# Four vector passes instead of five for the softmax exponentials that VectorE computes, 277 such score blocks instead of 228, and new pacing constants

## The chip, the cores and the metric

The kernel runs on one core of a Trainium2 chip. The core's engines are called as in its profile: PE (TensorE, matrix products; its weight loads are listed apart as PEld), ACT (ScalarE), DVE (VectorE), POOL (GpSimd) and SP (SyncE, which here only issues DMAs and waits). Each engine works through its own instructions in order and waits on semaphores for the others. The metric is the device time of one execution in microseconds (us); lower is better.

## The reference, cut to what matters

Two independent parts share one launch, and their outputs stand side by side.

```
# part A: attention, S = 2048, D = 512, 32 heads of 16
qkv = x @ wqkv                      # split in q, k, v per head
p = softmax(q @ k^T * 16 ** -0.5)   # 32 heads x 2048 x 2048
a = concat_heads(p @ v) @ wo

# part B: H3 block, D = 512 channels
kv = (4-tap causal shift of k with shift_k) * v
y  = causal convolution of kv with ssm_k, length 2048 per channel, + kv * ssm_D
b  = q * y
out = concat([a, b], axis=-1)
```

Part A needs 32 x 2048 x 2048 exponentials, 134 million. Part B is a long convolution for each of 512 channels.

## The kernel before, in words

**Score blocks.** A block is 128 keys x 512 queries of one head, so there are 2048 blocks. They are ordered in 32 groups of 64 (16 key tiles times four heads that sit in four 32-row strips of PE). Scores are written to PSUM by `qk_mm` (L675), one matmul per block; the queries are scaled beforehand so that a score x in PSUM means an exponential of 2 to the power x / 128. PSUM has eight banks of 512 fp32 columns: banks 0 to 5 hold scores, one block each, bank 6 (`PVB`) collects the product of the exponentials with V for the running group, bank 7 (`BGB`) serves everything else.

**Steps.** The main loop counts steps T. In even steps the score blocks go to the lower banks and in odd steps to the upper ones, mostly three banks each. `emit_qk` writes the scores of a step; `emit_exp` makes one ACT instruction of all its blocks (L708), which reads two or three neighbouring banks and writes bf16 exponentials to `PT`, a ring of 18 blocks. `pv_step` multiplies the blocks of step T-2 with V (L791), four at a time in the four strips of PE. A bank is free again once ACT has read it.

**Blocks on DVE.** `dve_block` (L719) decides in each step with at least three banks whether one of its blocks goes to DVE instead of ACT. It refuses while the work that waits on DVE is above `BACKLOG` us (5.8), while the fixed-point buffer of four blocks ago is in use, or near the end of a group, where 2.6 x `GAP` is the limit in blocks; there it may take a block of the next group. Such a step's ACT instruction has two banks and not three. `exp_on_dve` (L744) writes the passes, each one instruction on 128 x 512:

- L750: `fx = min(x + FIX_ADD, FIX_HI)`, fp32, PSUM to SBUF. The sum is placed so that its low 16 bits are the fraction f of the exponent, scaled by 2^16, and its value is, to first order, the bit pattern of the bf16 exponential. After it the PSUM bank is free.
- L757, three times: `eh = (eh + A) * f`, the steps of Horner's rule for a quartic in f that corrects the first order; in the first of them `eh` is f itself, read as uint16.
- L762: `PTD = eh * A4 + fx`, written as uint16, which is the bf16 exponential's bits. `PTD` is a ring of five blocks.

The passes after L750 wait in a list, `flow`. `advance` takes from it, in DVE's order, whatever the plan holds to be ready, and at most two blocks' passes are interleaved, so that a pass need not follow directly on the one whose result it reads. Other DVE work is `urgent`: it is put in when its input is due, and `slack` (`S_FX` for L750, 0.45) says how far listed passes may still go ahead of it.

**The convolution.** For each channel PE multiplies shifted windows of the kernel's taps (`WR`) with the values `KV`. Four channels (a quad) take 16 lags of four small matmuls each (`conv_lags`, L961); there are 128 quads, 2048 lags and 8192 matmuls. The windows of a quad are 2 MB, read from a scratch array in HBM by four DMAs on SP's queue, into a ring of four quads: 268 MB in all. The load into a ring place is issued when PE is done with the quad before. `emit_bg` puts lags between the steps' other work: each step adds to an allowance `PACE` x (lags left) / (time left by the plan), held below `RATE` per us and in sum below `CAP`; no more than `LAGS` = 6 are issued in one step, none past the room that PE has before the next scores are due, and a quad is begun only when the plan has its windows landed 1.5 us before (`WAIT`). In the rest of PE's room `warm_up` issues matmuls on zeros (L1166), which keep PE busy and compute nothing.

**The plan.** The whole order of work is fixed when the program is written: each `Eng` keeps a model of its time, `PLAN` (710) is the number of steps that due times are reckoned by, and the other projections (queries, keys, values, the output product) are `jobs` with due steps. On the chip only semaphores hold.

## Time and profile before

Three runs took 840.17, 843.98 and 844.13 us, median 843.98. The profiled execution has a span of 840.8 us from its first to its last instruction; no time of its own beyond the span is listed for it, and the span lies 0.6 us above the fastest run and 3.2 below the median.

| Engine | busy us | share of the span | instructions |
|---|---|---|---|
| ACT | 825.8 | 98% | 726 |
| DVE | 814.7 | 97% | 1392 |
| PE | 792.8 | 94% | 13774 |
| PEld | 333.3 | 40% | 13774 |
| POOL | 77.6 | 9% | 155 |

Busy time counts every moment in which an instruction is under way. Two neighbouring instructions overlap a little, so the duration of one is longer than the distance from its start to the next one's. PE's 792.8 us contain 162.4 us of the matmuls on zeros. The DMA engines moved 291.42 MB, 347 GB/s over the span.

### The profile page before, as it was taken

Reading aid. Unit: us, or ns where it says so; the run is one execution under the profiler, and the core shown is the slowest. Engines: PE = TensorE matmul, PEld = TensorE weight load, DVE = VectorE, ACT = ScalarE, POOL = GpSimd, SP = SyncE. Lnnn points to the kernel's source line nnn. Section 1 sums busy time; section 2 is a strip of 40 time slices with the busy share of each in tenths; the row PEclk is TensorE's granted clock in tenths of the full one; section 3 lists DMA queues with packets and bytes.
Section 4 is the critical chain, followed back from the end, with each engine's and each line's share of the span. In section 5 each row is a group of like instructions: output and inputs, shape, how many; then the busy total and the mean of one; then the engine's idle time right before and its main releaser. Section 6 shows DMA issues by size and latency. Waiting matters only on the chain.

```text
span 840.8 us, 30758 instructions
## 1 busy us (share of the span) xinstructions
PE 792.8 (94%) x13774; PEld 333.3 (40%) x13774; DVE 814.7 (97%) x1392; ACT 825.8 (98%) x726; POOL 77.6 (9%) x155
## 2 busy tenths in 40 slices
PE   8999999999999999999999999999999999999997
PEld 3343334444343434344434334443433333333442
DVE  3999999999999999999999999999999999999996
ACT  6999999999999999999999999999999999999997
POOL 3200220010100101000110010101002020000000
PEclk9999999999999999999999999999999999999999
DMA  9997199999999999999999999999999999999952
GB/s 230 216 310 285 50 371 370 354 347 408 392 408 394 393 402 338 371 326 378 330 379 408 384 340 359 377 405 398 406 408 379 351 394 409 409 316 391 405 200 76
DMA packets 109235, 291.42 MB, mean 347 GB/s; under 512 B 37680, under 2 KB 41648, under 8 KB 108720
## 3 DMA queue, kind: packets, MB, share of 16 engines
q1 hardware_dynamic: 102256, 280.80, 90.6%
q0 software_dynamic: 5648, 8.27, 3.2%
q8 instruction: 109, 1.79, 0.9%
q10 hardware_dynamic: 1200, 0.39, 0.2%
q14 instruction: 22, 0.18, 0.1%
HBM read 276.83 MB, written 6.42 MB: 337 GB/s over the span
## 4 chain that ended last, share of the span: by engine, by line
ACT 92%; PE 3%; DVE 3%; DMA 1%; issue 0%
ACT PT L708 92%; DVE EH L757 2%; PE PS L675 1%; PE PS L791 1%; DMA xT<-in_A_x_dram 1%; PE PS L961 1%; DVE PTD L762 1%; DVE FX L750 1%; PE PS L536 0%; PE PS L415 0%; PE PS L1166 0%; DVE DT L852 0%; ACT QT L920 0%; DVE DTN L863 0%; PE PS L902 0%
## 5 line engine op out<-in xcount | busy, mean ns | idle before, releaser
L708 ACT ACTIVATE PT<-PS 128x1536 bf16<-128x1536 f32 (+2 forms) x721 | 822.9, 1455 | 2.6 <-PE PS L675 2.6
L675 PE MATMUL PS<-QT,KTo 32*128 32x512 bf16 x2048 | 286.6, 384 | 34.6 <-ACT PT L708 6.6
L757 DVE SCALAR_TENSOR_TENSOR EH<-EH,FX 128x512 f32<-128x512 f32 x456 | 305.1, 687 | 0.0
L961 PE MATMUL PS<-WR,KV 128*15 128x128 bf16 (+15 forms) x8192 | 213.4, 219 | 1.1 <-issue 1.1
L791 PE MATMUL PS<-PT,VA 128*32 128x512 bf16 x1820 | 196.8, 389 | 2.0 <-DVE DT L852 0.6
L961 PEld LDWEIGHTS PS<-WR,KV 128*1 128x1 bf16 (+15 forms) x8192 | 144.7, 87 | 82.3 <-issue 47.1
L675 PEld LDWEIGHTS PS<-QT,KTo 32*128 32x128 bf16 x2048 | 72.7, 91 | 234.4 <-ACT PT L708 185.3
L1166 PE MATMUL PS<-IDN,ZW 128*32 128x512 bf16 (+4 forms) x632 | 162.4, 335 | 0.2
L750 DVE TENSOR_SCALAR FX<-PS 128x512 f32<-128x512 f32 x228 | 156.9, 690 | 2.4 <-PE PS L675 1.3
L762 DVE SCALAR_TENSOR_TENSOR PTD<-EH,FX 128x512 uint16<-128x512 f32 x228 | 155.7, 685 | 0.0
L757 DVE SCALAR_TENSOR_TENSOR EH<-FX 128x512 f32<-128x512 uint16 x228 | 155.7, 689 | 0.0
L259 POOL DMA_DIRECT2D QT<-QS x120 | 58.7, 497 | 481.5 <-DVE QS L442 165.7
L791 PEld LDWEIGHTS PS<-PT,VA 128*32 128x32 bf16 x1820 | 47.5, 93 | 108.6 <-issue 97.7
L791 PE MATMUL PS<-PTD,VA 128*32 128x512 bf16 x228 | 68.3, 383 | 0.3 <-DVE PTD L762 0.3
L1166 PEld LDWEIGHTS PS<-IDN,ZW 128*32 128x32 bf16 (+1 forms) x632 | 52.6, 96 | 23.8 <-issue 6.7
L852 DVE STREAM_TRANSPOSE DT<-PS 128x512 f32<-128x512 f32 x32 | 22.9, 716 | 6.2 <-PE PS L791 5.9
L975 DVE CAST YB<-PS 128x512 bf16<-128x512 f32 x32 | 22.0, 688 | 0.8 <-PE PS L961 0.8
L426 PE MATMUL PS<-WKV,xT 128*128 128x128 bf16 x256 | 18.8, 220 | 1.0 <-DVE KTo L451 0.7
L902 PE MATMUL PS<-WKV,OTN 128*128 128x512 bf16 x64 | 19.2, 384 | 0.3 <-DVE OTN L872 0.3
L403 PE MATMUL PS<-xT,WKV 128*128 128x512 bf16 (+1 forms) x64 | 18.1, 377 | 0.6 <-DVE KTo L451 0.5
L791 PEld LDWEIGHTS PS<-PTD,VA 128*32 128x32 bf16 x228 | 17.0, 95 | 2.0 <-DVE PTD L762 0.6
L394 PE MATMUL PS<-xT,WQ 128*128 128x512 bf16 x60 | 17.6, 384 | 0.2 <-DVE VA L473 0.2
(63 smaller groups left out, 211.8 us busy)
## 6 DMA issues: line engine op xcount, KB each, us to landing
WR<-kz_scratch SPq DMA_DIRECT2D x512, 512.0 KB, 8.0
kz_scratch<-WR SPq DMA_DIRECT2D x1, 2176.0 KB, 8.3
QN<-in_B_q_dram POOLq DMA_DIRECT2D x2, 1024.0 KB, 12.6
out_dram<-QN POOLq DMA_DIRECT2D x2, 1024.0 KB, 8.5
QT<-QS POOLq DMA_DIRECT2D x120, 16.0 KB, 5.2
out_dram<-OUTA POOLq DMA_DIRECT2D x12, 128.0 KB, 5.8
QN<-in_B_ssm_k_dram SPq DMA_DIRECT2D x1, 1024.0 KB, 8.5
OTN<-in_B_ssm_k_dram SPq DMA_DIRECT2D x1, 1024.0 KB, 9.1
```

The costliest lines, as they stand in the source:

```text
L259: f(outp, inp).then_inc(dsem.sem, 16)
L675: ins = e.matmul(PS[:, bank, :], lhsT=KTo[32 * s:32 * s + 32, OF[n_] % 2, kt * 128:(kt + 1) * 128], rhs=QT[32 * s:32 * s + 32, n_ // 2 % R ...
L708: h_exp[T] = act.op(lambda e: e.activation(PT[:, p0:p0 + n, :].rearrange("p b f -> p (b f)"), PS[:, banks[0]:banks[0] + n, :].rearrange("p ...
L750: h_f = urgent(lambda e: e.tensor_scalar(fx, PS[:, bank, :], FIX_ADD, FIX_HI, ALU.add, ALU.min), [h, h_last.get(i - R_FX)], slack=S_FX)
L757: st["h"] = dve.op(lambda e: e.scalar_tensor_tensor(eh, src, (A3, A2, A1)[j], frac, ALU.add, ALU.mult), [st["h"], h_last.get(i - R_EH)], u ...
L762: lambda e: e.scalar_tensor_tensor(out16, eh, A4, fx, ALU.mult, ALU.add),
L791: ins = e.matmul(dst, lhsT=w, rhs=rhs, start=(k == 0), stop=(k == KT - 1), tile_position=(0, 32 * s))
L852: h_t = urgent(lambda e: e.transpose(out=dt, in_=PS[:, PVB, :]), [h, h_mul.get(n - 1)], slack=S_T, us=(0.63, 0.751))
L902: ins = e.matmul(PS[:, bank, :], lhsT=OTN[:, PAIRS.index((o, qb)), t * 128:(t + 1) * 128], rhs=WO[:, o, :], start=(o == 0), stop=(o == 3))
L961: ins = e.matmul(PS[32 * c:32 * c + NB - n, BGB, 128 * (kk % 4):128 * (kk % 4) + 128], lhsT=KV[:, qd, n:NB, c], rhs=WR[:, r + c, 128 * (NB ...
L975: hh = urgent(lambda e: e.tensor_copy(YB[:, half, :].rearrange("p (k i) -> p k i", k=4), src), [h, h_yb[0]], slack=S_C, us=V512)
L1166: pe.op(lambda e, s=s, k=k, rhs=rhs, bank=bank, rows=rows, c0=c0, first=first: e.matmul(PS[32 * s:32 * s + rows, bank, c0:c0 + 128 * k], l ...
```

## The change

Horner's quartic becomes two nested quadratics: `y = (f + P1) * f`, `z = (y + P2) * y`, `PTD = z * P3 + fx`. So L757 is issued twice per block and not three times, and a block has four DVE passes and not five. In the second of them both operands and the result are `eh`. ACT's bias moves by 5.016e-5. With the shorter chain and the new constants of the plan, the program gives DVE 277 blocks instead of 228 and ACT the other 1771 instead of 1820. The convolution's allowance grows faster (`PACE`, `RATE`) and may be saved up further (`CAP`); `LAGS`, the most in one step, stays at 6. The other constants touched belong to the plan: how late L750 may come (`S_FX`), the reckoned number of steps (`PLAN`), the limit near a group's end (`GAP`), and the work that may wait on DVE (`BACKLOG`).

```diff
-PACE = 1.05
+PACE = 1.2
...
-EXP_BIAS = (LIFT + 1) * math.log(2.0)
...
-A3, A2, A1 = 255023.64843928182, 77186915383.44943, -6435437372016724.0
-A4 = 9.315941845433171e-20
+P1 = 7.78027265 * 2.0 ** 16
+P2 = -8.78027265 * 2.0 ** 32
+P3 = 4.46542389e-3 * UNIT / 2.0 ** 64
+EXP_BIAS = (LIFT + 1) * math.log(2.0) + 5.016e-5
...
-S_FX = 0.45
+S_FX = 0.55
...
-PLAN = 710
+PLAN = 705
...
-GAP = 8
+GAP = 7
...
-BACKLOG = 5.8
+BACKLOG = 6.0
...
-RATE = 3.4
-CAP = 10.0
+RATE = 3.7
+CAP = 14.0
...
-        def horner(j, us):
+        def square(j, us):
             src = frac if j == 0 else eh
-            st["h"] = dve.op(lambda e: e.scalar_tensor_tensor(eh, src, (A3, A2, A1)[j], frac, ALU.add, ALU.mult),
+            st["h"] = dve.op(lambda e: e.scalar_tensor_tensor(eh, src, (P1, P2)[j], src, ALU.add, ALU.mult),
                              [st["h"], h_last.get(i - R_EH)], us=us)
...
-                lambda e: e.scalar_tensor_tensor(out16, eh, A4, fx, ALU.mult, ALU.add),
+                lambda e: e.scalar_tensor_tensor(out16, eh, P3, fx, ALU.mult, ALU.add),
...
-        flow.append([("p", dep, lambda us: horner(0, us), V512,
-                      lambda: i < R_EH or i - R_EH in h_last)]
-                    + [("p", dep, lambda us, j=j: horner(j, us), V512, lambda: True) for j in (1, 2)]
-                    + [("p", dep, last, V512, lambda: i < R_PTD or i - R_PTD in h_ptd)])
+        flow.append([("p", dep, lambda us: square(0, us), V512,
+                      lambda: i < R_EH or i - R_EH in h_last),
+                     ("p", dep, lambda us: square(1, us), V512, lambda: True),
+                     ("p", dep, last, V512, lambda: i < R_PTD or i - R_PTD in h_ptd)])
```

## The prediction, made before the result was known

> **What bounds the kernel now.** I read the busy shares first, then the chain that ended last, then the groups of instructions by shape, then who waited for whom, and last the stretches of 20 us.

> The page's busy shares and its chain:

> ```profile
> span 840.8 us, 30758 instructions
> PE 792.8 (94%) x13774; PEld 333.3 (40%) x13774; DVE 814.7 (97%) x1392; ACT 825.8 (98%) x726; POOL 77.6 (9%) x155
> ...
> ACT 92%; PE 3%; DVE 3%; DMA 1%; issue 0%
> ```

> ACT carries 92% of the chain. DVE, at 97%, is nearly as full, so both must be counted.

> The groups, shapes kept apart (count, busy us, mean ns, idle before and its releaser):

> ```profile
> L708 ACT ACTIVATE PT<-PS 128x1536 bf16<-128x1536 f32 x372 | 575.2, 1663 | 0.7 <-PE PS L675 0.7
> L708 ACT ACTIVATE PT<-PS 128x1024 bf16<-128x1024 f32 x346 | 395.4, 1229 | 0.4 <-PE PS L675 0.4
> L757 DVE SCALAR_TENSOR_TENSOR EH<-EH,FX 128x512 f32<-128x512 f32 x456 | 305.1, 687 | 0.0
> ...
> L750 DVE TENSOR_SCALAR FX<-PS 128x512 f32<-128x512 f32 x228 | 156.9, 690 | 2.4 <-PE PS L675 1.3
> L762 DVE SCALAR_TENSOR_TENSOR PTD<-EH,FX 128x512 uint16<-128x512 f32 x228 | 155.7, 685 | 0.0
> L757 DVE SCALAR_TENSOR_TENSOR EH<-FX 128x512 f32<-128x512 uint16 x228 | 155.7, 689 | 0.0
> L1166 PE MATMUL PS<-IDN,ZW 128*32 128x512 bf16 x360 | 115.8, 380 | 0.0
> ```

> The reader sees 372 activations of three blocks, 346 of two (three more have four), and five DVE passes per block that all last about the same, whatever they read.

> DVE's order of time, 662 us into the run (start, duration):

> ```profile
> 661.62 0.68 DVE L762 SCALAR_TENSOR_TENSOR PTD<-EH,FX 128x512 uint16<-128x512 f32 x1
> 662.21 0.69 DVE L757 SCALAR_TENSOR_TENSOR EH<-EH,FX 128x512 f32<-128x512 f32 x1
> 662.82 0.69 DVE L757 SCALAR_TENSOR_TENSOR EH<-FX 128x512 f32<-128x512 uint16 x1
> ```

> A pass lasts 0.69 us but the next starts 0.60 us after it: 0.60 is the price of a pass.

> The waits of PE and ACT (us in total, times, longest):

> ```profile
> PEld PS L675 <- ACT PT L708: 185.3, 483, 0.9
> ...
> ACT PT L708 <- PE PS L675: 2.6, 5, 1.5
> ```

> PE waits for ACT 185.3 us, to get a score bank back; ACT waits for PE 2.6. Together with 162.4 us of matmuls on zeros, PE has some 350 us that the plan can give away.

> Stretches of 20 us (PE, PEld, DVE, ACT, POOL busy, granted clock, DMA share, GB/s):

> ```profile
> 480.00:500.00 20.00, 19.42 (x294) 7.17 (x286) 19.95 (x34) 20.00 (x20) 3.88 (x8) 1.00 0.99 353
> ...
> 700.00:720.00 20.00, 19.29 (x359) 7.87 (x356) 19.85 (x36) 20.00 (x19) 1.08 (x2) 1.00 1.03 409
> ...
> 800.00:820.00 20.00, 18.91 (x366) 8.11 (x360) 19.85 (x35) 20.00 (x18) 0.00 (x0) 1.00 0.47 184
> ```

> ACT is solid in all of them; the DMA engines are busy throughout too, with 353 to 409 GB/s, and the convolution's loads end only after 800 us.

> **The change, part by part.** The sum is made against the profiled execution: span 840.8 us, with 9.7 us ahead of the first L708 and 7.1 after the last (it ends at 833.7). Neither end is touched.

> *ACT loses 49 blocks.* From the start times of L708 in the trace, a two-block activation is followed after 904 ns and a three-block one after 1331 (medians), so a block costs 427 ns and an activation 50 ns besides. Before: 1820 x 0.427 + 721 x 0.050 = 777.1 + 36.1 = 813.2 us. The stretch from first to last L708 is 824.0, so 10.7 us are small gaps, in 18 places over 0.15 us and many tiny ones. After: 1771 x 0.427 = 756.2. The number of activations should stay near 721, since a block on DVE takes its bank out of an activation and leaves the step. Bounds: 5 steps fewer, as the reckoned 705 instead of 710 has it, is -0.25 us; 49 steps more, were every further DVE block to keep its bank a step longer, is +2.4. I take 721, nearest to the present mix. ACT: 49 x 0.427 = -20.9 us, all on the path.

> *The gaps.* Two-block activations exceed 904 ns by 23 ns on average, three-block ones 1331 by 7.5. With 49 of the threes turned into twos: 395 x 0.023 + 323 x 0.0075 = 11.5 us, +0.8. Bounds: all gaps gone, -10.7; doubled, since 21 us less of PE's slack remain and the convolution comes in larger portions, +10.7. I take +0.8, because ACT's waits for PE, 2.6 us, are small against 350 us of slack.

> *DVE has 277 x 4 = 1108 passes instead of 228 x 5 = 1140.* 32 fewer at 0.60 us is -19.2. L750, L762 and the first L757 keep their operands; the second L757 reads `eh` on both inputs and writes it, and no row shows one fp32 tensor on both inputs. The nearest rows bound it: L757 with `eh` as input and output, 687 ns, and L757 with f on both inputs, 689. I take 0.60 and bound it by 0.58 and 0.62, the neighbours' spread, 277 x 0.02 = 5.5 us each way. DVE's busy time becomes 795.5. Now it idles 26.1 us: 12.8 in the first 20 us, 7.7 in the last 20.8, 5.6 in between. With the ends kept, DVE alone would need 795.5 + 20.5 = 816.0 us, 4 to 5 less than ACT's path, so it stays second but close. If the pass took 0.62, DVE would need 821.5, about ACT's time.

> *S_FX, GAP, BACKLOG.* L750 may start up to 0.1 us later, so a bank comes back 0.1 us later in at most 277 steps. What hides it: DVE holds its bank while ACT reads two others for 904 ns and then the next step's for at least as long. Without that cover it is 28 us; who waited for L750 in the trace was PE's weight load, 2.7 us in 6 places, so I take 0. GAP lets DVE take blocks 2.6 blocks (about one step) later in a group; a group's closing product then waits for them, behind it the transpose L852, which waited 5.9 us in all. Priced with the gaps above.

> *The convolution.* The lags, their matmuls and the 512 loads stay; only their places move. A quad needed 5.67 us before (first lag 93.6, last 820.3, 128 quads). The span shorter by 20, it must come down to about 5.52. Where loads follow each other closest they land 5.06 to 5.15 us apart per quad, so it fits, by 7%. What the larger allowance takes on PE comes out of L1166 and PE's waits. PE reads no window that has not landed: the smallest distance from landing to first use was 2.8 us, the median 6.6, and no wait of PE names these loads. SP's queue only waits for ring places and issues (0.43 us each), so earlier lags mean earlier issues. POOL's queue, with 120 issues of the queries' copies, gets a busier DMA; these land in 5.2 us (at most 7.9) and are due 24 steps, some 27 us, ahead: nothing.

> [...]

> *Sum.* -20.9 + 0.8 = -20.1 us: 820.7 us against the span. The median lay 3.2 us above the span, so the same difference gives 823.9. I take the middle, 822: two of the three runs were high, the profiled one and the third low. ACT is still first, DVE 4 us behind it.

> **The rivals.**
> 1. *The gaps double.* PE gets shorter steps (904 ns more often) and portions of up to 6 lags more often, and DVE has less than 5 us of idle time inside; each late bank delays ACT. For it: between 194 and 219 us the chain already runs along DVE's passes. Against: the solid ACT rows. 822 + 10.7 = 833.
> 2. *The gaps go.* The new plan might avoid the late places. 822 - 10.7 = 811. Nothing in the profile speaks for it.
> 3. *The windows can't come faster.* From the first issue at 51.4 to the last landing at 810.9 us the loads' mean was 353 GB/s; if troughs such as 480 to 500 us belong to the stream and can't be filled, the last landing stays where it is, and 30 us later the kernel ends: 841 to 844, no change. Against: from 80 to 100 us the DMA engines idle, the ring being full, and 409 GB/s are reached. [...]
> 4. *Slower: PE stalls on windows.* The plan now asks for up to 1.2 x 2048 lags over 708 us, 3.47 per us, more than the 16 per 5.1 us, 3.14, that land at best. So early quads are begun as soon as the plan holds them to be landed. If they land later than planned, PE stops in order, with the next scores behind it, and ACT after about one step. It decides where the stop costs ACT 20.1 / 124 = 0.16 us per quad; at 0.3 us the time is 822 + 37 = 859. Against: the 2.8 us of smallest distance, in stretches where the loads were already back to back.
> 5. *The change does not take hold:* DVE can't carry more than 228 blocks in time, and ACT waits for what it was spared. About 843. Against: 1108 passes are fewer than 1140.

> **How the numbers follow.** The forecast has 0.77; rivals 1 to 5 have 0.11, 0.03, 0.03, 0.04 and 0.02. The forecast's own range is 816 (half of the gaps gone) to 828 (half again as many, on the high kind of run). To leave out no more than 2 in 10 it must reach the doubled gaps: 816 to 833. Half a per cent, 4.2 us, is about what a measurement of this kernel can tell from no change, its runs being 4 us apart. Faster: forecast and rivals 1 and 2, 0.91; within: 3 and 5, 0.05; slower: 4, 0.04.

> **What would show it.** Right: L708 with about 721 instructions, some 395 of them two-block, and some 802 us busy; L757 with 277 + 277 instructions at 0.69 us; ACT still about 92% of the chain; L1166 shrunk by up to 20 us; the last L961 near 800 us or before. Wrong: L961 waiting for `WR` loads, ACT's idle time before L708 above 15 us, L708 counts well above 721, or a second L757 longer than 0.71 us.

## The result and the profile after

The changed kernel takes 833.7 us (median of 4 runs, 827.86 to 834.92), the kernel before 842.96 (4 runs); the ratio is 0.9886, 95% interval 0.985 to 0.9923. So the change makes the kernel faster by 1.1%, 9.3 us, where 822 us and 816 to 833 were forecast. The profiled execution has a span of 832.3 us and took 834.01 in all.

The page of the changed kernel: shares, and the chain that ended last.

```profile
span 832.3 us, 30664 instructions
PE 773.8 (93%) x13668; PEld 327.7 (39%) x13668; DVE 794.8 (95%) x1360; ACT 808.2 (97%) x730; POOL 78.5 (9%) x155
...
ACT 69%; PE 15%; DVE 11%; issue 3%; DMA 2%; POOL 0%; DVEq 0%
```

DVE's 794.8 us were forecast as 795.5. But ACT's part of the chain has fallen from 92% to 69%, and PE, DVE and "issue" stand in its place.

The groups of the changed kernel, shapes kept apart (busy us, mean ns, idle before and releaser):

```profile
L709 ACT ACTIVATE PT<-PS 128x1536 bf16<-128x1536 f32 x316 | 482.0, 1579 | 8.7 <-PE PS L676 8.6
L709 ACT ACTIVATE PT<-PS 128x1024 bf16<-128x1024 f32 x405 | 429.9, 1167 | 3.2 <-PE PS L676 2.7
...
L758 DVE SCALAR_TENSOR_TENSOR EH<-EH 128x512 f32<-128x512 f32 x277 | 186.4, 686 | 0.0
L758 DVE SCALAR_TENSOR_TENSOR EH<-FX 128x512 f32<-128x512 uint16 x277 | 186.3, 689 | 0.0
```

There are 725 activations (three of four blocks and one of a single block besides these). With the same start-to-start times as before (904 and 1331 ns) they need 792.5 us, 20.7 less than before; -20.9 was forecast. The pass that reads `eh` twice lasts 686 ns like every other. The gaps between activations, though, have grown from 10.7 to 24.4 us:

| From 840.8 to 832.3 us of span | us |
|---|---|
| ACT's work, start to start | -20.7 |
| gaps between activations | +13.7 |
| earlier first activation (8.1 instead of 9.7 us) | -1.6 |

The sum, -8.6, is the difference of the spans to 0.1. The first activation came between 8.0 and 10.0 us in the profiles of all kernels here (8.1 in one that differs from the kernel before in its windows alone), so I take the third row for chance. The question is where the 13.7 us come from.

Waits of the changed kernel (us, times, longest):

```profile
ACT PT L709 <- PE PS L676: 12.4, 18, 2.1
...
PE PS L962 <- issue: 10.7, 11, 2.0
```

ACT waits for the scores, and PE, in the midst of its convolution (now L962), for nothing that the profile names. Such a place, in order of time:

```profile
234.80 0.09 PEld L792 LDWEIGHTS PS<-PT,VA 128*32 128x32 bf16 x1 [0.23 <-issue]
...
236.49 0.40 PE L792 MATMUL PS<-PT,VA 128*32 128x512 bf16 x4 [1.62 <-issue]
...
237.43 3.83 ACT L709 ACTIVATE PT<-PS 128x1536 bf16<-128x1536 f32 x3 [0.74 <-PE PS L676]
```

PE loads the first of four weights and then stands still for 1.62 us, inside a group of matmuls of which only the first waits on a semaphore. The next scores come late, ACT idles 0.74 us.

In PE's order of instructions (matmuls, weight loads and its few separate waits, numbered from 0) these places have something in common. The list has every pause over 0.35 us ahead of an instruction that waits on nothing, and the packet of the DMA queue of kind "instruction", 16384 bytes each, that ended before it:

```
pause ends  us    number  mod 256   packet start  end     end to resume
187.85     0.90    5313     193        185.41    186.50      1.35
207.78     0.43    6081     193        205.43    206.54      1.24
236.49     1.60    7105     193        233.93    235.01      1.48
270.97     0.90    8385     193        268.45    269.55      1.43
277.89     1.55    8641     193        275.23    276.31      1.57
406.25     0.85   13505     193        404.03    404.97      1.28
494.57     2.04   16321     193        492.15    493.12      1.45
547.84     0.44   18113     193        545.45    546.59      1.25
554.35     1.72   18369     193        552.05    553.02      1.33
588.02     0.84   19649     193        585.50    586.60      1.43
595.26     0.73   19905     193        592.76    593.84      1.43
```

All eleven (12.0 us) lie at one place of a period of 256 instructions, and each ends 1.2 to 1.6 us after such a packet. A twelfth, 0.84 us at 485 us, lies at the same border ahead of a waiting instruction. The kernel before has three, 1.7 us in all, also at 193 of 256. My reading, which the experiments below test: PE had used up its instructions and waited for the next block of 256, which such a packet brings. The counts in the trace agree: 108 packets of 16384 bytes on that queue, and PE has 27682 instructions, 108 times 256 and 34 more.

By this reading the block that comes is fetched while the running one is used up: a packet starts 3.4 us (median; 95% below 4.9, longest 6.3) after PE enters a block and takes 1.1, and at the pauses above PE goes on 1.4 us later. From the entry that is 5.8 us in the median, while a block lasts 6.95 us (median). Where lags are dense it lasts less: without its pause, under 6 us in 24 cases (with 22.6 lags in the mean, the other blocks with 18.1), before in 8.

After the longest pause PE was also slow, in the stretch behind the pause that ended at 494.57 (PE, PEld, DVE, ACT, POOL, granted clock, DMA share, GB/s):

```profile
496.00:500.00 4.00, 4.00 (x75) 1.79 (x67) 1.79 (x3) 3.02 (x3) 0.00 (x0) 0.61 0.93 266
```

The granted clock was 0.61 in these 4 us, and ACT lost another 1.2 us. From 424 to 428 us it was 0.57, after PE had stood still for 2.4 us for another cause (below, the queries' copies). Behind the other pauses it stayed at 1.00.

With that, ACT's 24.4 us of gaps can be told apart by place. At the twelve border places, each counted from the pause's begin to 2.2 us after its end, they are 10.5 us; between 419 and 430 us 3.1; in the slow stretch behind 496 us 1.2. Outside these places 9.6 us are left. In the kernel before, its three border places have 1.3 us, and 9.4 lie elsewhere.

### The profile page after: what moved, and what is told of

The parts are those of the page before. It is cut to its first block, busy times and chain, and to the rows that moved or that the text cites. A ratio compares the mean times of both kernels' runs of the same rounds, so it can differ in the third digit from the quotient of the medians.

```text
span 832.3 us, 30664 instructions
## 1 busy us (share of the span) xinstructions
PE 773.8 (93%) x13668; PEld 327.7 (39%) x13668; DVE 794.8 (95%) x1360; ACT 808.2 (97%) x730; POOL 78.5 (9%) x155
## 2 busy tenths in 40 slices
DMA packets 109235, 291.41 MB, mean 350 GB/s; under 512 B 37680, under 2 KB 41648, under 8 KB 108720
## 4 chain that ended last, share of the span: by engine, by line
ACT 69%; PE 15%; DVE 11%; issue 3%; DMA 2%; POOL 0%; DVEq 0%
ACT PT L709 69%; PE PS L676 5%; DVE EH L758 4%; PE PS L962 3%; PE PS L792 3%; DVE FX L751 3%; DVE PTD L763 2%; PE PS L1167 1%; DMA QT<-QS 1%; DMA QN<-in_B_k_dram 1%; DMA xT<-in_A_x_dram 1%; PE PS L427 0%; DVE DT L853 0%; POOL QT L260 0%; PE PS L395 0%
## 5 line engine op out<-in xcount | busy, mean ns | idle before, releaser
L709 ACT ACTIVATE PT<-PS 128x1024 bf16<-128x1024 f32 (+2 forms) x725 | 805.2, 1349 | 12.9 <-PE PS L676 12.4
L962 PE MATMUL PS<-WR,KV 128*15 128x128 bf16 (+15 forms) x8192 | 213.0, 220 | 10.8 <-issue 10.7
L751 DVE TENSOR_SCALAR FX<-PS 128x512 f32<-128x512 f32 x277 | 189.1, 689 | 8.6 <-PE PS L676 8.0
L763 DVE SCALAR_TENSOR_TENSOR PTD<-EH,FX 128x512 uint16<-128x512 f32 x277 | 187.5, 685 | 0.1
L758 DVE SCALAR_TENSOR_TENSOR EH<-EH 128x512 f32<-128x512 f32 x277 | 186.4, 686 | 0.0
L758 DVE SCALAR_TENSOR_TENSOR EH<-FX 128x512 f32<-128x512 uint16 x277 | 186.3, 689 | 0.0
L962 PEld LDWEIGHTS PS<-WR,KV 128*15 128x15 bf16 (+15 forms) x8192 | 143.4, 88 | 86.6 <-issue 56.0
L1167 PE MATMUL PS<-IDN,ZW 128*32 128x512 bf16 (+4 forms) x517 | 134.5, 328 | 0.3 <-DVE DT L853 0.2
L792 PE MATMUL PS<-PTD,VA 128*32 128x512 bf16 x277 | 81.3, 383 | 0.3 <-DVE PTD L763 0.3
L1167 PEld LDWEIGHTS PS<-IDN,ZW 128*32 128x32 bf16 (+1 forms) x517 | 43.3, 96 | 26.2 <-issue 11.1
L792 PEld LDWEIGHTS PS<-PTD,VA 128*32 128x32 bf16 x277 | 20.1, 95 | 2.0 <-DVE PTD L763 0.6
L404 PE MATMUL PS<-xT,WKV 128*128 128x512 bf16 (+1 forms) x64 | 18.4, 378 | 1.0 <-DVE KV L462 0.5
```

Of the source, the lines that this page charges most:

```text
L709: h_exp[T] = act.op(lambda e: e.activation(PT[:, p0:p0 + n, :].rearrange("p b f -> p (b f)"), PS[:, banks[0]:banks[0] + n, :].rearrange("p ...
L751: h_f = urgent(lambda e: e.tensor_scalar(fx, PS[:, bank, :], FIX_ADD, FIX_HI, ALU.add, ALU.min), [h, h_last.get(i - R_FX)], slack=S_FX)
L758: st["h"] = dve.op(lambda e: e.scalar_tensor_tensor(eh, src, (P1, P2)[j], src, ALU.add, ALU.mult), [st["h"], h_last.get(i - R_EH)], us=us)
L763: lambda e: e.scalar_tensor_tensor(out16, eh, P3, fx, ALU.mult, ALU.add),
L792: ins = e.matmul(dst, lhsT=w, rhs=rhs, start=(k == 0), stop=(k == KT - 1), tile_position=(0, 32 * s))
L962: ins = e.matmul(PS[32 * c:32 * c + NB - n, BGB, 128 * (kk % 4):128 * (kk % 4) + 128], lhsT=KV[:, qd, n:NB, c], rhs=WR[:, r + c, 128 * (NB ...
```

## The experiments

Three theories were tried. Theory 1: PE's instructions come late, because their fetch queues behind the convolution's windows in the DMA engines and because denser lags use up a block faster. Theory 2: the shorter steps are too tight for PE, DVE and the banks. Theory 3: PE waits for windows that land late. In the figures below, pauses are those of the list above (over 0.35 us, ahead of an instruction without a wait), and gaps are ACT's, over the start-to-start times.

**Half of the windows' traffic, on the changed kernel**

```diff
-            for c in range(4):
+            for c in range(2):
...
-                h_wr[qd] = dma(sp, d_wr[i], WR[:, 4 * i + c, :], src, [h_kzw[0], dep])
+                h_wr[qd] = dma(sp, d_wr[i], WR[:, 4 * i + c, :], src, [h_kzw[0], dep], kb=1024)
...
-                                   rhs=WR[:, r + c, 128 * (NB - 1 - n):128 * (NB - n)],
+                                   rhs=WR[:, r + c % 2, 128 * (NB - 1 - n):128 * (NB - n)],
```

> The changed kernel, but of each quad's four channels only two have their windows loaded (two DMAs of 512 KB instead of four), and the other two channels' matmuls read those same windows; so half of the convolution is not the reference's, while every engine's instructions and their order stay as in the changed kernel. Theory 1 (PE runs out of instructions: the fetch of its next 256 waits in the DMA engines behind the windows): the gaps of PE inside a group of matmuls, 12.8 us in 12 places, fall below 3 us, the fetch's packet starts well under 3 us after PE enters the block before, and the time falls from 833.7 to 820 to 824. Theory 2 (the plan is too tight on PE and DVE, late banks delay ACT): the stream of windows has nothing to do with it, the time stays at 832 to 835. Theory 3 (PE waits for windows that land late): faster as well, 820 to 826; e3 tells it from theory 1.

823.88 us (ratio to the kernel before 0.9761, 0.9722 to 0.98). The DMA traffic of this kernel:

```profile
DMA packets 72369, 157.16 MB, mean 191 GB/s; under 512 B 33584, under 2 KB 37552, under 8 KB 71856
```

and its chain that ended last, by engine:

```profile
ACT 91%; PE 3%; DVE 3%; DMA 1%; issue 1%
```

The fetch's packet starts 1.1 us after PE enters a block (median) instead of 3.4. (43 matmuls are missing in this trace, so PE's instructions were counted by the weight loads, which are complete.) Two pauses are left, 2.1 us, again at 193 of 256, and gaps of 14.0 us. ACT has its 91% of the chain again. That is theory 1's or 3's; theory 2 falls for 10 of the 13.7 us. The gap of 3.1 us at the queries' copies is gone too, so not all of the 10 is the fetch's.

**The same on the kernel before**

The edit is the same.

> The kernel before with the same halving of the windows (two of a quad's four channels loaded, the others read the same). It says what the halving is worth where there is little to cure. Theory 1: PE's gaps inside a group of matmuls were 1.7 us in 3 places and go; the time falls by 1 to 3 us, to 839 to 842. Theory 2: no change, 842 to 844. Theory 3: no change either, since no window landed less than 2.8 us ahead of its use.

840.16 us, ratio 0.9972 (0.9953 to 0.9992): 2.4 us faster by the interval's middle, no pause left, gaps 9.8. Taking the traffic away helps little where blocks were seldom late, so most of the 10 us of the first experiment was the change's own loss.

**Half of the convolution's matmuls, all of the traffic**

```diff
             for n in range(n0, n1):
-                for c in range(4):
+                for c in range(2):
```

> The changed kernel with all windows loaded, but with the convolution's matmuls of two of the four channels left out (8192 to 4096; the four run side by side in PE's strips, so the plan's times stand; half of the convolution's output is missing). PE's instructions fall by some 8192 of 27700. Theory 1: PE needs 256 new instructions less often (mean block time from 7.0 to some 10 us) and the fetch is in time though the DMA engines are as busy as before: gaps inside a group below 2 us, time 820 to 824. Theory 2: what is tight is ACT, DVE and the order of steps, which stay: 830 to 835. Theory 3: the windows land no earlier, so PE waits for them as before: 832 to 835.

822.71 us (ratio 0.975, 0.9709 to 0.9791). This kernel's DMA traffic:

```profile
DMA packets 109203, 290.89 MB, mean 354 GB/s; under 512 B 37680, under 2 KB 41648, under 8 KB 108720
```

and its wait for windows (us, times, longest):

```profile
PEld PS L962 <- DMA WR<-kz_scratch: 8.9, 13, 1.8
```

The DMA engines move as much as in the changed kernel (291.41 MB there) and more per second (350 GB/s there). PE even waits for windows in 13 places, which it did not in the changed kernel. Still there is no pause of the list's kind, 76 packets are fetched instead of 108, a block lasts 10.2 us (median), and the time is 11 us lower. That speaks against theory 3 for the changed kernel and for theory 1: with the same traffic, fewer instructions suffice.

**The new pace alone, on the kernel before**

```diff
-PACE = 1.05
+PACE = 1.2
...
-RATE = 3.4
-CAP = 10.0
+RATE = 3.7
+CAP = 14.0
```

> The kernel before (five passes, 228 blocks) with only the convolution's new pace (PACE 1.2, RATE 3.7, CAP 14). Theory 1: the lags come in denser portions and the DMA engines are full earlier, so PE's blocks of 256 instructions are used up faster and their fetch comes later: gaps inside a group of matmuls rise from 1.7 to 4 to 10 us, and the time from 843 to 846 to 851. Theory 2: the steps stay long and DVE's work the same, so the time stays at 841 to 844. Theory 3: windows are used sooner after landing, 0.5 to 3 us; slower only if PE's waits end with a landing.

849.19 us, ratio 1.0078 (1.0054 to 1.0102): the time that theory 1 expected, but not for its reason. There is one pause, 0.4 us. PE's wait for windows:

```profile
PE PS L961 <- DMA WR<-kz_scratch: 6.9, 6, 3.5
```

Here it is theory 3: the windows are used so soon after landing that PE waits for them, 5.4 of the 6.9 us between 428 and 448 us, where 1 MB of the convolution's output goes out on POOL's queue between its issue at 433.4 and 445.1. ACT's gaps are 17.7 instead of 10.7 us. So the denser pace costs time by itself, through either of two transfers in the same DMA engines (90% busy or more in 34 of the page's 40 slices here, in 35 in the changed kernel); through which, depends on the kernel that it is put in.

**The four passes alone, DVE held to 227 blocks**

All constants as before, and in `dve_block`:

```diff
+        if i >= 228 * T / 715:
+            return None
```

> The four passes alone: the changed kernel's formula with all constants of the plan as before and DVE held to 227 blocks, ACT having 1821. The forecast's first step says that time goes only with ACT's blocks: L708 stays at 813 us of starts plus 10 to 12 of gaps, DVE idles some 130 us more, and the time stays at 840 to 845. Rival: DVE's 97% was itself a bound, late passes caused the gaps, and with 227 passes fewer the gaps shrink: 830 to 836.

845.63 us, ratio 1.0041 (1.0019 to 1.0063), 0.6 us outside what was expected. Shares:

```profile
PE 787.9 (93%) x13786; PEld 330.3 (39%) x13786; DVE 711.3 (84%) x1160; ACT 827.1 (98%) x727; POOL 78.7 (9%) x155
```

DVE has 103 us less to do and nothing is gained: DVE was no bound, and the gain is in ACT's 49 blocks. That it is 3.5 us slower goes with gaps of 14.3 us. The pauses are three, 2.2 us, little more than before. A wait of DVE for the copies of the queries, 6.3 us in 2 places, is among the causes of the gaps; the rest was not followed.

**Two of the three pace constants set back, on the changed kernel**

```diff
-RATE = 3.7
-CAP = 14.0
+RATE = 3.4
+CAP = 10.0
```

> The changed kernel with two of the convolution's three constants set back (RATE 3.4, CAP 10; PACE stays at 1.2, since with 1.05 besides the lags no longer end before the last steps). Theory 1: PE's blocks of 256 instructions are used up a little more slowly, but still often in less than 6 us; gaps at a block's border 5 to 11 us instead of 12, time 827 to 833. Theory 3 (windows): they are used a little later after landing, nothing else: 831 to 835.

831.37 us (0.9865, 0.9836 to 0.9894); seven pauses, 6.5 us, all at the border; gaps 18.4. The time lies in the ranges of theory 1 and theory 3 alike, and its runs (830.28 to 832.09) lie within those of the changed kernel, so only the pauses and gaps speak, and for theory 1: a little less dense, a little less lost.

**A plan that counts PE's instructions**

On top of the last kernel:

```diff
+FETCH = 5.8
+FETCH_AT = 191
+FETCH_REST = 15.0
...
+        if self.ins is not None:
+            c = Count()
+            fn(c)
+            k = (self.ins - FETCH_AT) // 256
+            self.ins += c.n + max(len(waits) - 1, 0)
+            if (self.ins - FETCH_AT) // 256 > k:
+                self.entered = self.t
...
+        soon = pe.entered + FETCH - pe.t
+        if soon > 0:
+            left = min(left, int((256 - (pe.ins - FETCH_AT) % 256 - FETCH_REST * soon) / 8))
```

`Count` calls a group's function with matmuls that only count two instructions each, one for the weights. A lag has eight, and the plan reckons 15 per us for all other work.

> As e6, and the plan counts PE's instructions: for 5.8 us after PE enters a block of 256 it issues no more lags than leave enough of the block for the other work until then. DMA traffic, DVE's and ACT's blocks stay (277 and 1771). Theory 1: the fetch is in time nearly always; gaps at a block's border below 3 us, ACT's gaps 12 to 16 us in all, time 819 to 825, faster than both kernels. Theory 2 (the plan is tight on banks and DVE): as e6, 827 to 835.

824.58 us, ratio 0.9781 (0.9746 to 0.9816), faster than both kernels, and 6.8 us below the kernel without the count, on the same chip (the two profiled executions are 4.5 us apart, 3.7 of it ACT's gaps). DVE has 277 blocks, where the kernel without the count has 276. One block of 256 instructions lasts under 6 us, where the changed kernel had 24, and there is no pause. Its groups of activations (busy us, mean ns, idle before):

```profile
L734 ACT ACTIVATE PT<-PS 128x1536 bf16<-128x1536 f32 x317 | 492.2, 1625 | 1.2 <-PE PS L701 1.1
L734 ACT ACTIVATE PT<-PS 128x1024 bf16<-128x1024 f32 x404 | 439.0, 1201 | 2.7 <-PE PS L701 2.2
```

ACT's wait for the scores (us, times, longest), which was 12.4 us in the changed kernel:

```profile
ACT PT L734 <- PE PS L701: 5.0, 8, 1.7
```

Two of its stretches (PE, PEld, DVE, ACT, POOL, granted clock, DMA share, GB/s):

```profile
260.00:280.00 20.00, 19.23 (x384) 8.16 (x383) 19.94 (x36) 20.00 (x19) 3.81 (x8) 1.00 1.03 399
...
540.00:560.00 20.00, 18.23 (x385) 7.89 (x386) 19.88 (x36) 20.00 (x18) 0.00 (x0) 1.00 1.03 408
```

The same stretches of the changed kernel:

```profile
260.00:280.00 20.00, 16.97 (x354) 7.45 (x345) 17.78 (x32) 18.60 (x18) 3.82 (x8) 1.00 1.03 394
...
540.00:560.00 20.00, 17.33 (x375) 7.91 (x372) 18.66 (x33) 18.40 (x17) 1.90 (x4) 1.00 1.02 375
```

ACT is solid (20.00) where it had lost 1.4 and 1.6 us, with the DMA engines as full. ACT's gaps are 14.7 us.

**PACE alone set back, on the changed kernel**

```diff
-PACE = 1.2
+PACE = 1.05
```

> The changed kernel with PACE alone set back to 1.05 (RATE 3.7, CAP 14 stay). The allowance grows more slowly while many lags are left, but what is saved up can still be spent six at a time. Theory 1: fewer short blocks, gaps at a block's border 4 to 10 us, time 826 to 832. Theory 3: windows are used 1 to 3 us later after landing than in the changed kernel, no wait names them in either, time as the changed kernel's, 831 to 835.

831.28 us (0.9876, 0.9829 to 0.9923), in the ranges of theory 1 and theory 3 alike; the pauses are fewer than theory 1 said, four with 2.5 us, and the gaps are 20.2. Some 4.5 us of them lie between 421 and 428, at one place where the queries' copies come late (below). Its runs (828.93 to 835.28) overlap those of the changed kernel almost wholly, so this run tells little.

Pauses and gaps side by side:

| Kernel | pauses | us | ACT's gaps, us | median us |
|---|---|---|---|---|
| before | 3 | 1.7 | 10.7 | 842.96 |
| changed | 11 | 12.0 | 24.4 | 833.7 |
| before, half the windows | 0 | 0 | 9.8 | 840.16 |
| before, new pace | 1 | 0.4 | 17.7 | 849.19 |
| four passes, 227 blocks | 3 | 2.2 | 14.3 | 845.63 |
| changed, half the windows | 2 | 2.1 | 14.0 | 823.88 |
| changed, half the matmuls | 0 | 0 | 14.7 | 822.71 |
| changed, RATE and CAP as before | 7 | 6.5 | 18.4 | 831.37 |
| the same, instructions counted | 0 | 0 | 14.7 | 824.58 |
| changed, PACE as before | 4 | 2.5 | 20.2 | 831.28 |

Pauses are one cause of gaps among several: the new pace on the kernel before adds its gaps through late windows, and in the last row 4.5 us come from the queries' copies.

## Why the prediction failed, point by point

- *ACT loses 49 blocks, -20.9 us:* right, -20.7. The number of activations, 725 instead of the 721 taken, lies between the bounds, and two-block ones are 405 instead of 395.
- *DVE, second by 4 to 5 us, the new pass at 0.60:* right; 794.8 us busy, the pass 686 ns, and with 227 blocks it idles without any gain.
- *The gaps, +0.8 us:* this step failed. They grew by 13.7, beyond the upper bound of 10.7. The reason given, 350 us of PE's slack against 2.6 us of ACT's waits, counts PE's time, and counts it too high: the 185.3 us are idle time of the weight loads, and in 159 of them PE's matmuls run. PE's own wait for ACT in the kernel before is this:

```profile
PE PS L675 <- ACT PT L708: 6.6, 24, 0.6
```

  PE idled 48.0 us in all, so its slack was nearer to 210 us, still plenty. What ran out was PE's supply of instructions, of which a lag needs eight in 55 ns of the plan's time: 10.5 us of gaps lie at the borders, 1.3 before. Rival 1 had the time, 833, and the wrong mechanism: it put the loss on late banks, short steps and portions of lags. Of these only the portions show a part, through the instructions; outside the places named the gaps are as before, 9.6 and 9.4 us.
- *The convolution, "what the larger allowance takes on PE comes out of L1166 and PE's waits":* true of time (L1167 is down to 134.5 from 162.4 us busy), and the step that should have had a price: packing the same lags more densely cost instruction fetches in time. The profile of before held the sign. In its chain, in order of time, there are three pieces put down to nothing:

```profile
192.05 0.44 issue
...
410.35 0.60 issue
...
617.21 0.64 issue
```

  They belong to the three pauses of before. Pauses that the profile can't name, on the engine whose instructions were to be packed more densely, had to be followed to their place in the order.
- *The queries' copies, "nothing":* wrong by 3.1 us, at one place, and not by the 24 steps that were counted. The chain of the changed kernel:

```profile
411.44 3.33 POOL QT L260 x7
414.77 6.72 DMA QT<-QS
```

  The copies read the one buffer `QS`, and DVE's next pass into it (L443) must wait for them: they landed at 421.49, L443 began at 421.62, and the next scores waited for L443. ACT had a gap of 2.3 us there and 0.9 in the slower clock after it. In the kernel before L443 came 2.4 us after the landing.
- *Rival 3, windows that can't come faster:* did not happen; the last landed at 795.7 instead of 810.9 us, and stretches of 20 us reach 409 GB/s again.
- *Rival 4, PE stalls on windows:* not in the changed kernel, where they landed 0.4 us or more ahead of their use (before 2.8), but in the kernel before with the new pace, where it costs most of 7 us of gaps. The price per quad was right in kind; the margin of 2.8 us was no margin of that other order.
- *The median against the span:* the profiled execution took 1.7 us more than its span, and that of the halved windows 1.7 too. So the profile before stood for some 842.5, near the median, and not for the low end. Counting from the span plus 1.7 would have given 822.4 for the same sum, no other answer.

What stays open: the kernels with few pauses or none still have gaps of 14 to 15 us and not 10.7 to 11.5. With half the windows 3.3 us of them lie around the two pauses left, and with half the matmuls 3.0 behind PE's waits for windows. With the instructions counted, 1.5 us lie right behind the first activation, and 2.9 in and around two stretches from 467 and 669 us, where the granted clock was 0.50 for 3.3 us though PE had not stood still for more than 1.2 us at once. Why the clock fell there, and why the second activation came late, none of the runs tells.

## What to carry to other kernels

PE had, in the kernels here, a budget of instructions beside its budget of time. Where another edit shortens the time, or packs small instructions more densely, compare the time of 256 instructions (here 7.0 us) with the time that their fetch takes under the DMA load of that stretch (here 5.8, with the latest packet some 8.8). Pauses inside a group without a wait, which the profile calls "issue", are to be numbered in the engine's order; here a common remainder, 193 of 256 in all eleven of the changed kernel and all three of the one before, gave the fetch away (where a trace lacks matmuls, the numbers come from the weight loads). The cure here was in the order: a count of instructions in the plan won 6.8 us with the same traffic and all but the same work.
